# Where TensorE's idle transposes begin in a planned attention and MoE kernel, and separate order weights for its first and last units

## The chip, the cores and the metric

The kernel runs on one core of one Trainium2 chip. The core has a matrix engine (TensorE, PE), a vector engine (VectorE, DVE), an activation engine (ScalarE, ACT), a general engine (GpSimd, POOL) and an engine that here only issues transfers (SyncE, SP). The metric is the device time of one execution in microseconds. Three runs of the kernel before gave 693.09, 693.29 and 693.81 us, a median of 693.29.

## The reference

The computation is an attention whose queries are averaged in twos, followed by two MLPs without residuals. Everything is float32. The weights of the exponent are sharp, since q and k are scaled up by about 6 each.

```python
# q, k, v: (2, 8, 1152, 64)
q_pool = q.reshape(B, H, S // 2, 2, D).mean(axis=3)
scores = np.matmul(q_pool, k.transpose(0, 1, 3, 2)) / np.sqrt(D)
attn = np.exp(scores - scores.max(-1, keepdims=True))
attn = attn / (attn.sum(-1, keepdims=True) + 1e-09)
x = merge_heads(np.matmul(attn, v))                        # (1152, 512)
g = x @ w_gate                                             # d_ff 1536
x = (g * sigmoid(g) * (x @ w_val)) @ w_out
h = x @ w_in                                               # d_ff 2048
out = (np.maximum(h, 0) + alpha * np.minimum(h, 0)) @ w_out2
```

## The kernel before

**Numbers in two parts.** To keep float32's accuracy, every operand of a matmul is split into a high part (rounded to the type that PE multiplies at speed) and a low part (the rest). A product is then two or three matmuls. For the attention the splits are made on ACT, DVE and POOL; for the weights of the MLPs, `weights` (line 363) loads 1024 columns and runs seven steps on them: two on ACT (lines 376 and 381) and five on DVE (lines 377 to 380 and 382).

**Attention.** The 16 heads are handled as 8 pairs. A pair has 1152 pooled query rows, in 9 units of 128 (unit 4 holds the last rows of one head and the first of the other). For a unit, `unit` (line 513) computes scores against all 1152 keys, in three pieces of 448, 448 and 256 columns (line 542, PE), takes the row maximum on DVE (lines 551 and 552) and the exponents on ACT (lines 554 and 556). `transposed` (line 565) turns the exponents in three blocks of 384 with PE transposes (line 583). Each block is then split: either by ACT (line 605, high part) and DVE (line 606, low part), or, for every third block, by an ACT copy (line 591) and POOL (lines 601 and 602). `values` (line 611) multiplies with v (line 623), and `finish` (line 643) scales by the inverse sums and writes the attention's output in two parts, `xh` and `xl`. `prep` (line 402) loads and splits q, k and v for a pair. For the first pair it loads q in two pieces and k in three; q's second piece is needed from unit 2 on.

**MLPs.** `contract` (line 702) multiplies a block of weights with 384 tokens (line 710); then follow gating or the leaky step, and the output products (lines 770 and 798). Work of the first MLP on the first tokens needs only pairs 0 to 3, so it can run while the last pair of the attention is still under way.

**The order of the work.** Nothing of this order stands in the loops. Every piece of work is a task with an engine, an assumed duration and a priority, and `Plan.run` (line 122) plays the program through once while it is being built: each engine takes the ready task with the lowest priority number whose buffers have a place, and the instructions are emitted in that order. At run time each engine keeps that order and waits by semaphores. Priorities count four per pair: unit `n` of pair `p` has position `4p + 4(n + 0.5)/9`, and to it an offset from the dictionary `KNOB` (line 24) is added: `qk` for scores, `max` for the maxima, `exp` for the exponents, `t` for the transposes, `hi` and `lo` for the parts, `v` for the products, `prep` and `fin` for a pair's begin and end. Tasks of a weight block have the priority `max(clock - lead, floor)`, where the clock starts at 33 behind the last pair. `begin` names the unit of the last pair before whose transposes no weight of the MLPs is loaded. The `hold` numbers say how long an engine may stay idle for a more urgent task that is nearly ready.

**Idle transposes.** Ahead of the plan, PE does 21 transposes of the identity matrix (line 286). In the plan, as long as the planned time is under 40 us and no product has begun, a PE that has nothing ready does one more such transpose (line 289), for which the plan counts 0.109 us:

```python
free = {PE: 0.0, ACT: 0.0, DVE: 0.0, POOL: 1.7, SP: 0.6}
...
if e == PE and free[e] <= now + 1e-9 and now < 40.0 and not self.classes["acc"]["next"]:
    self.idle()
    free[e] = now + tp(P)
```

PE's planned time begins at 0. The 21 transposes ahead of the plan are not counted in it.

## Time and profile before

| | us |
|---|---|
| median of three runs | 693.29 |
| the profiled execution | 692.54 |
| its span (first to last instruction) | 690.7 |
| PE busy | 680.7 (99%) |
| DVE busy | 524.4 (76%) |
| ACT busy | 391.1 (57%) |
| POOL busy | 216.1 (31%) |

The profile is that of one execution. Its times start at the span's start. "Busy" on PE includes transposes that compute nothing, and matmuls are pipelined, so that PE's busy time covers small gaps. PEld is the loading of weights into PE, which overlaps the matmuls. A row of a timeline names a start, a duration, an engine, a line, an operation and, in brackets, how long the engine was idle before and for whom.

### The profile page before, as it was taken

The page shows a single profiled execution, that of the slowest core. Times are in us where ns is not written, and L with a number is a line of the kernel's source. Part 1 is how long each engine was busy: PE and PEld are TensorE (multiplying, and loading weights), DVE is VectorE, ACT ScalarE, POOL GpSimd, SP SyncE. Part 2 cuts the span into 40 slices and gives each one's busy share as a digit, 9 for nine tenths or more (in the row PEclk, how much of TensorE's full clock was granted, in tenths as well). Part 3 has the DMA queues.
Part 4 walks back from the last instruction along what each step waited for, and adds up shares of the span by engine and source line. Part 5 has one row for each costly group of instructions (what it writes and reads, how often), then busy time and mean ns, then how long its engine had stood idle before and what let it go on. Part 6 is the DMA issues. An engine that isn't in the chain of part 4 may idle for free.

```text
span 690.7 us, 11125 instructions
## 1 busy us (share of the span) xinstructions
PE 680.7 (99%) x4108; PEld 640.7 (93%) x4108; DVE 524.4 (76%) x900; ACT 391.1 (57%) x833; POOL 216.1 (31%) x246
## 2 busy tenths in 40 slices
PE   9999999999999989999999999999999999999997
PEld 8899999999999979999999999998999998999886
DVE  3798988889889899999775696659699559663432
ACT  2888889998998985545433442231376464342210
POOL 2879698898987751000000000004200000000000
PEclk9999999999999999999999999999999999999999
DMA  6665566664664233434331132013113303000012
GB/s 184 173 135 145 135 163 167 156 156 118 158 154 112 89 124 140 164 139 156 139 134 62 61 122 86 38 61 122 62 62 122 122 1 121 1 1 1 1 47 91
DMA packets 21655, 72.99 MB, mean 106 GB/s; under 512 B 3096, under 2 KB 4064, under 8 KB 21600
## 3 DMA queue, kind: packets, MB, share of 16 engines
q1 hardware_dynamic: 21312, 71.92, 34.3%
q8 instruction: 32, 0.52, 0.3%
q10 hardware_dynamic: 288, 0.36, 0.1%
q14 instruction: 23, 0.19, 0.1%
HBM read 52.17 MB, written 2.40 MB: 79 GB/s over the span
## 4 chain that ended last, share of the span: by engine, by line
PE 89%; DVE 8%; POOL 1%; issue 1%; ACT 0%; DVEq 0%; POOLq 0%
PE bank L710 35%; PE bank L798 14%; PE bank L542 12%; PE bank L583 10%; PE bank L623 10%; PE bank L770 7%; PE bank L289 1%; DVE fed L606 1%; POOL xh L779 1%; DVE plain L777 1%; DVE magnitudes L379 1%; DVE stats L551 1%; DVE weights L382 1%; DVE magnitudes L377 1%; DVE xl L780 1%
## 5 line engine op out<-in xcount | busy, mean ns | idle before, releaser
L710 PE MATMUL bank<-xh,weights 128*128 128x384 f32 x960 | 253.5, 337 | 0.5 <-DVE plain L777 0.3
L710 PEld LDWEIGHTS bank<-xh,weights 128*128 128x128 f32 x960 | 174.4, 188 | 2.4 <-issue 0.6
L710 PE MATMUL bank<-xl,weights 128*128 128x384 f32 x480 | 161.4, 336 | 0.0
L623 PE MATMUL bank<-fed 128*128 128x256 f32 (+1 forms) x576 | 109.5, 310 | 1.0 <-POOL fed L602 0.6
L583 PE MATMUL bank<-ident,plain 128*128 128x128 f32 x648 | 102.3, 275 | 2.1 <-DVE fed L606 1.4
L798 PE MATMUL bank<-fed 128*128 128x512 f32 x432 | 102.6, 389 | 0.0
L542 PE MATMUL bank<-fed 128*128 128x448 f32 (+3 forms) x396 | 100.9, 360 | 0.4 <-ACT plain L556 0.4
L606 DVE TENSOR_TENSOR fed<-bank,fed 128x384 fp32r<-128x384 f32 (+1 forms) x176 | 82.1, 496 | 16.2 <-ACT fed L605 14.7
L798 PEld LDWEIGHTS bank<-fed 128*128 128x128 f32 x432 | 80.6, 188 | 14.9
L710 PEld LDWEIGHTS bank<-xl,weights 128*128 128x128 f32 x480 | 90.2, 188 | 1.0
L583 PEld LDWEIGHTS bank<-ident,plain 128*128 128x128 f32 x648 | 76.4, 140 | 12.7 <-DVE fed L606 5.8
L623 PEld LDWEIGHTS bank<-fed 128*128 128x128 f32 x576 | 84.2, 189 | 3.2 <-POOL fed L602 1.0
L551 DVE TENSOR_REDUCE stats<-bank 128x1 f32<-128x896 f32 x72 | 78.1, 1085 | 10.2 <-PE bank L542 9.1
L605 ACT ACTIVATE fed<-bank 128x384 fp32r<-128x384 f32 (+1 forms) x176 | 72.2, 453 | 16.2 <-PE bank L583 15.7
L770 PE MATMUL bank<-fed 128*128 128x384 f32 x432 | 80.3, 337 | 0.9 <-DVE plain L777 0.8
L770 PEld LDWEIGHTS bank<-fed 128*128 128x128 f32 x432 | 75.6, 188 | 2.4 <-DVE plain L777 2.4
L779 POOL TENSOR_SCALAR xh<-plain 128x384 fp32r<-128x384 f32 x12 | 12.3, 1027 | 207.8 <-DVE plain L777 207.8
L556 ACT ACTIVATE plain<-bank,stats 128x896 f32<-128x896 f32 x72 | 73.1, 1015 | 0.3
L602 POOL TENSOR_TENSOR fed<-plain,fed 128x384 fp32r<-128x384 f32 x64 | 71.5, 1118 | 5.3
L542 PEld LDWEIGHTS bank<-fed 128*128 128x128 f32 (+1 forms) x396 | 63.2, 189 | 5.9 <-ACT plain L556 2.1
L750 ACT ACTIVATE plain<-bank,signs 128x384 f32<-128x384 f32 x48 | 28.0, 582 | 68.3 <-PE bank L710 68.3
L751 DVE SCALAR_TENSOR_TENSOR plain<-bank,signs,plain 128x384 f32<-128x384 f32 x48 | 29.4, 615 | 36.3 <-ACT plain L750 36.3
(73 smaller groups left out, 838.4 us busy)
## 6 DMA issues: line engine op xcount, KB each, us to landing
fed<-fed SPq DMA_DIRECT2D x60, 288.0 KB, 3.4
plain<-in_w_out SPq DMA_DIRECT2D x28, 512.0 KB, 4.1
plain<-in_w_in SPq DMA_DIRECT2D x16, 512.0 KB, 4.3
plain<-in_w_gate SPq DMA_DIRECT2D x12, 512.0 KB, 3.4
plain<-in_w_val SPq DMA_DIRECT2D x12, 512.0 KB, 4.6
plain<-in_vt SPq DMA_DIRECT2D x8, 576.0 KB, 5.8
plain<-in_qt SPq DMA_DIRECT2D x7, 576.0 KB, 7.2
plain<-in_kt SPq DMA_DIRECT2D x7, 576.0 KB, 7.6
```

The lines of the kernel that those rows point to most:

```text
L542: nc.tensor.matmul(bank[:, banks[i], :js.stop - js.start], l(), r(js), start=a == 0, stop=a == len(terms) - 1)
L551: add(DVE, dve(2 * WIDE), lambda: nc.vector.tensor_reduce(m(1), two(), AX.XY, ALU.min), pos + K["max"], [(sa, 0), (sa, 1)], [(st, 1)], [sa ...
L556: add(ACT, act(2 * WIDE, acc=True), lambda: nc.scalar.activation(e.ap[:, :2 * WIDE].rearrange("p (a b) -> p a b", a=2), two(), AF.Exp, bia ...
L583: nc.tensor.transpose(t.ap[:, c * P:c * P + P], e.ap[:, ks:ks + P], ident)
L602: add(POOL, gp2(BLK * w), lambda cp=cp, to=to, cols=cols: nc.gpsimd.tensor_tensor(to(1), src3(cp.ap)[:, :, cols], to(0).bitcast(F32), ALU. ...
L605: add(ACT, act(BLK * w), lambda t=t, to=to, cols=cols: nc.scalar.activation(to(0), src3(t.ap)[:, :, cols], AF.Copy), at + K["hi"], [t], [( ...
L606: add(DVE, dve(BLK * w), lambda t=t, to=to, cols=cols: nc.vector.tensor_tensor(to(1), src3(t.ap)[:, :, cols], to(0).bitcast(F32), ALU.subt ...
L623: nc.tensor.matmul(acc.ap[:, :n], v, b.ap[:, at:at + n], start=kc == 0 and part == 0, stop=kc == NK - 1 and part == 1)
L710: nc.tensor.matmul(acc.ap[:, :TB], l[:, cs], r[:, c, ts], start=c == 0 and a == 0, stop=c == KC - 1 and a == 2)
L751: add(DVE, dve(TB) + 0.056, lambda: nc.vector.scalar_tensor_tensor(u.ap, a.ap[:, :TB], sign(), u.ap, ALU.mult, ALU.max), prio, [a], [u], [ ...
L770: nc.tensor.matmul(acc.ap[:, :TB], l[:, os_], r, start=n == 0 and m == 0, stop=n == len(g) - 1 and m == 2)
L798: nc.tensor.matmul(acc.ap, l, r, start=n == 0 and m == 0, stop=n == len(g) - 1 and m == 2)
```

## The change

- PE's planned time begins at 5.0 (`first`) instead of 0.0.
- A function `turn` gives the tasks of unit 0 of pair 0 (`ramp=1`), and of unit 8 of the last pair (`last=1`), an extra offset in the order (`qk0` and so on, `qk9` and so on). The products have an extra offset for the first two groups of pair 0 (`v0`) and for the last two groups of the last pair (`v9`).
- In the last pair, POOL takes every second block instead of every third (`pool9=2`, `pooln=9`).
- The low part of the first `wlo` weight blocks can be made on POOL; `wlo` is 0.
- The base offsets and holds of `KNOB` have new values, among them `exp` (1.119 to 1.755), `lo` (-4 to -1.847), `begin` (1 to 0), `lead` (2.5 to 5.556) and `floor` (32.203 to 32.61).

```diff
--- before.py
+++ after.py
@@ -21,7 +21,7 @@
-KNOB = dict(qk=-1.541, max=-1.328, exp=1.119, t=-0.493, hi=-1.499, lo=-4, v=1.588, prep=-0.504, fin=0.163, hold_pe=0.2, hold_act=0.017, hold_dve=0, hold_pool=0.228, pvn=1, begin=1, lead=2.5, floor=32.203, warm=21, wide=448, tb=(5, 6, 2), ab=(7,), pool=3, e=3, et=6, wc=3, wr=4, h=17)
+KNOB = dict(ramp=1, qk0=-0.057, max0=1.439, exp0=1.712, t0=-0.168, hi0=-0.613, lo0=1.449, v0=-0.09, last=1, qk9=-0.348, exp9=2.109, t9=-0.81, hi9=-0.422, lo9=-1.681, v9=-2.742, pool9=2, pooln=9, wlo=0, qk=-1.546, max=-1.339, exp=1.755, t=-0.488, hi=-1.801, lo=-1.847, v=1.584, prep=-0.593, fin=0.029, hold_pe=0.192, hold_act=0, hold_dve=0.009, hold_pool=0.13, pvn=1, begin=0, lead=5.556, floor=32.61, warm=21, wide=448, tb=(5, 6, 2), ab=(7,), pool=3, e=3, et=6, wc=3, wr=4, h=17)
 class Task:
@@ -51,6 +51,7 @@
     def __init__(self):
         self.tasks = []
         self.classes = {}
+        self.first = 5.0
         self.idle = None
         self.wr = {}
         self.rd = {}
@@ -122,7 +123,7 @@
     def run(self, hold):
         self.held = set()
-        free = {PE: 0.0, ACT: 0.0, DVE: 0.0, POOL: 1.7, SP: 0.6}
+        free = {PE: self.first, ACT: 0.0, DVE: 0.0, POOL: 1.7, SP: 0.6}
         wait = {e: [] for e in free}
         moved = 2.6
         events, seq = [], 0
@@ -360,6 +361,8 @@
     LEAST = 3.4332275390625e-05
+    made = [0]
+
     def weights(kind, srcs, prio):
         raw, mag, w = buf("raw"), buf("mag"), buf(kind)
         for i, src in enumerate(srcs):
@@ -379,7 +382,9 @@
         add(DVE, dve(2 * DM), lambda: nc.vector.scalar_tensor_tensor(bits(), word(0, I32), 29, bits(), ALU.logical_shift_right, ALU.bitwise_or), prio, reads=got, writes=[mag], bufs=[raw, mag])
         add(DVE, dve(2 * DM), lambda: nc.vector.scalar_tensor_tensor(bits(), word(1, I32), -0x40000000, bits(), ALU.bitwise_and, ALU.bitwise_or), prio, reads=got, writes=[mag], bufs=[raw, mag])
         add(ACT, act(2 * DM, True), lambda: nc.scalar.activation(hi(), mag.ap, AF.Copy), prio, reads=[mag], writes=[w], bufs=[mag, w])
-        add(DVE, dve(2 * DM), lambda: nc.vector.tensor_tensor(w.ap[:, 2 * DM:], mag.ap, hi().bitcast(F32), ALU.subtract), prio, reads=[mag], writes=[w], bufs=[mag, w])
+        made[0] += 1
+        lo, dur, eng = (POOL, gp2(2 * DM), nc.gpsimd) if made[0] <= K["wlo"] else (DVE, dve(2 * DM), nc.vector)
+        add(lo, dur, lambda: eng.tensor_tensor(w.ap[:, 2 * DM:], mag.ap, hi().bitcast(F32), ALU.subtract), prio, reads=[mag], writes=[w], bufs=[mag, w])
         return [(w, i) for i in range(len(srcs))]
     def whi(u):
@@ -401,6 +406,7 @@
     def prep(p):
         x = Pair()
+        x.p = p
         s0 = 4.0 * (p - 1) + K["prep"]
         first = p == 0
         x.qq, x.kk = [None, None], [None, None]
@@ -509,6 +515,15 @@
         return x
     count = [0]
+
+    def turn(kind, p, n):
+
+
+        if p == 0 and n < K["ramp"]:
+            return K[kind] + K.get(kind + "0", 0.0)
+        if p == NP - 1 and n >= 9 - K["last"]:
+            return K[kind] + K.get(kind + "9", 0.0)
+        return K[kind]
     def unit(x, p, n, pos):
@@ -543,18 +558,18 @@
         for i in range(3):
             s = sb if i == 2 else sa
-            add(PE, len(terms) * mm(CUTS[i][1] - CUTS[i][0]), lambda i=i: scores(i), pos + K["qk"], rd(CUTS[i]), [(s, i)], [s] + held)
+            add(PE, len(terms) * mm(CUTS[i][1] - CUTS[i][0]), lambda i=i: scores(i), pos + turn("qk", p, n), rd(CUTS[i]), [(s, i)], [s] + held)
         m = lambda i: st.ap[:, i:i + 1]
         sum_ = lambda i: x.sums.ap[:, i, n:n + 1]
         two = lambda: bank[:, first:first + 2, :WIDE]
         one = lambda: bank[:, 2, :S - 2 * WIDE]
-        add(DVE, dve(2 * WIDE), lambda: nc.vector.tensor_reduce(m(1), two(), AX.XY, ALU.min), pos + K["max"], [(sa, 0), (sa, 1)], [(st, 1)], [sa, st])
+        add(DVE, dve(2 * WIDE), lambda: nc.vector.tensor_reduce(m(1), two(), AX.XY, ALU.min), pos + turn("max", p, n), [(sa, 0), (sa, 1)], [(st, 1)], [sa, st])
         add(DVE, dve(S - 2 * WIDE) + 0.056, lambda: nc.vector.tensor_scalar(junk[:, :S - 2 * WIDE], one(), m(1), None, ALU.min, ALU.min, accum_out=m(0)),
-            pos + K["max"], [(st, 1), (sb, 2)], [(st, 0)], [sb, st])
+            pos + turn("max", p, n), [(st, 1), (sb, 2)], [(st, 0)], [sb, st])
         add(ACT, act(S - 2 * WIDE, acc=True), lambda: nc.scalar.activation(e.ap[:, 2 * WIDE:], one(), AF.Exp, bias=m(0), scale=-1.0, accum_out=sum_(0)),
-            pos + K["exp"], [(st, 0), (sb, 2)], [(e, 1), (x.sums, n, 0)], [sb, e, st, x.sums])
+            pos + turn("exp", p, n), [(st, 0), (sb, 2)], [(e, 1), (x.sums, n, 0)], [sb, e, st, x.sums])
         add(ACT, act(2 * WIDE, acc=True), lambda: nc.scalar.activation(e.ap[:, :2 * WIDE].rearrange("p (a b) -> p a b", a=2), two(), AF.Exp, bias=m(0), scale=-1.0, accum_out=sum_(1)),
-            pos + K["exp"], [(st, 0), (sa, 0), (sa, 1)], [(e, 0), (x.sums, n, 1)], [sa, e, st, x.sums])
+            pos + turn("exp", p, n), [(st, 0), (sa, 0), (sa, 1)], [(e, 0), (x.sums, n, 1)], [sa, e, st, x.sums])
         return e, [[(e, h) for h in range(2) if (i * TB < 2 * WIDE if h == 0 else (i + 1) * TB > 2 * WIDE)] for i in range(NBLK)]
@@ -582,13 +597,13 @@
                     ks = (i * BLK + c) * P
                     nc.tensor.transpose(t.ap[:, c * P:c * P + P], e.ap[:, ks:ks + P], ident)
-            add(PE, tp(BLK * P), tr, at + K["t"], etok[i], [t] + mark, [t, e])
+            add(PE, tp(BLK * P), tr, at + turn("t", p, n), etok[i], [t] + mark, [t, e])
             src3 = lambda ap: ap[:, :BLK * P].rearrange("p (c q) -> p c q", q=P)
             c0 = 0
-            by_pool = K["pool"] and blocks[0] % K["pool"] == 0 and n != 4
+            by_pool = n != 4 and (blocks[0] % K["pool"] == 0 if p < NP - 1 else n < K["pooln"] and blocks[0] % K["pool9"] == 0)
             if by_pool:
                 cp = buf("cp")
-                add(ACT, act(BLK * P), lambda t=t, cp=cp: nc.scalar.activation(cp.ap, t.ap[:, :BLK * P], AF.Copy), at + K["hi"], [t], [cp], [t, cp])
+                add(ACT, act(BLK * P), lambda t=t, cp=cp: nc.scalar.activation(cp.ap, t.ap[:, :BLK * P], AF.Copy), at + turn("hi", p, n), [t], [cp], [t, cp])
             for et, off, w, width in dst:
                 b = et[i]
@@ -598,19 +613,20 @@
                 cols = slice(c0, c0 + w)
                 if by_pool:
-                    add(POOL, gp(BLK * w), lambda cp=cp, to=to, cols=cols: nc.gpsimd.tensor_scalar(to(0), src3(cp.ap)[:, :, cols], 1.0, 1.0, ALU.mult, ALU.mult), at + K["hi"], [cp], [(b, off, 0)], [cp, b])
+                    add(POOL, gp(BLK * w), lambda cp=cp, to=to, cols=cols: nc.gpsimd.tensor_scalar(to(0), src3(cp.ap)[:, :, cols], 1.0, 1.0, ALU.mult, ALU.mult), at + turn("hi", p, n), [cp], [(b, off, 0)], [cp, b])
                     add(POOL, gp2(BLK * w), lambda cp=cp, to=to, cols=cols: nc.gpsimd.tensor_tensor(to(1), src3(cp.ap)[:, :, cols], to(0).bitcast(F32), ALU.subtract),
-                        at + K["lo"], [cp, (b, off, 0)], [(b, off, 1)], [cp, b])
+                        at + turn("lo", p, n), [cp, (b, off, 0)], [(b, off, 1)], [cp, b])
                 else:
-                    add(ACT, act(BLK * w), lambda t=t, to=to, cols=cols: nc.scalar.activation(to(0), src3(t.ap)[:, :, cols], AF.Copy), at + K["hi"], [t], [(b, off, 0)], [t, b])
+                    add(ACT, act(BLK * w), lambda t=t, to=to, cols=cols: nc.scalar.activation(to(0), src3(t.ap)[:, :, cols], AF.Copy), at + turn("hi", p, n), [t], [(b, off, 0)], [t, b])
                     add(DVE, dve(BLK * w), lambda t=t, to=to, cols=cols: nc.vector.tensor_tensor(to(1), src3(t.ap)[:, :, cols], to(0).bitcast(F32), ALU.subtract),
-                        at + K["lo"], [t, (b, off, 0)], [(b, off, 1)], [t, b])
+                        at + turn("lo", p, n), [t, (b, off, 0)], [(b, off, 1)], [t, b])
                 b.parts += [(b, off, 0), (b, off, 1)]
                 c0 += w
     def values(x, g, et, eo, xs, pos):
         j, q0, q1 = GROUPS[g]
         n = q1 - q0
+        later = K["v"] + (K["v0"] if x.p == 0 and g < 2 else K["v9"] if x.p == NP - 1 and g > 1 else 0.0)
         acc = buf("acc")
         for kc in range(0, NK, K["pvn"]):
             b = et[kc // BLK]
@@ -622,10 +638,10 @@
                         at = (part * BLK + kc % BLK) * n
                         nc.tensor.matmul(acc.ap[:, :n], v, b.ap[:, at:at + n], start=kc == 0 and part == 0, stop=kc == NK - 1 and part == 1)
-            add(PE, 2 * K["pvn"] * mm(n), pv, pos + kc * 0.007 + K["v"], b.parts + [(x.vs[j], 0), (x.vs[j], 1)], [acc], [acc, b, x.vs[j]])
+            add(PE, 2 * K["pvn"] * mm(n), pv, pos + kc * 0.007 + later, b.parts + [(x.vs[j], 0), (x.vs[j], 1)], [acc], [acc, b, x.vs[j]])
         mine, rest = (slice(0, D), slice(D, P)) if j == 0 else (slice(D, P), slice(0, D))
-        add(ACT, act(n) + 0.136, lambda: nc.scalar.activation(eo.ap[mine, q0:q1], acc.ap[rest, :n], AF.Copy), pos + K["v"], [acc], [(eo, g)], [acc, eo])
-        add(DVE, dve(n), lambda: nc.vector.tensor_tensor(xs.ap[mine, q0:q1], acc.ap[mine, :n], eo.ap[mine, q0:q1], ALU.add), pos + K["v"], [acc, (eo, g)], [(xs, g)], [acc, eo, xs])
+        add(ACT, act(n) + 0.136, lambda: nc.scalar.activation(eo.ap[mine, q0:q1], acc.ap[rest, :n], AF.Copy), pos + later, [acc], [(eo, g)], [acc, eo])
+        add(DVE, dve(n), lambda: nc.vector.tensor_tensor(xs.ap[mine, q0:q1], acc.ap[mine, :n], eo.ap[mine, q0:q1], ALU.add), pos + later, [acc, (eo, g)], [(xs, g)], [acc, eo, xs])
     def inverses(x, pos, rd):
```

## Rows read from the trace of the kernel before

**Rows 1.** The page: busy time, and the chain that ended last by engine.

```profile
PE 680.7 (99%) x4108; PEld 640.7 (93%) x4108; DVE 524.4 (76%) x900; ACT 391.1 (57%) x833; POOL 216.1 (31%) x246
...
PE 89%; DVE 8%; POOL 1%; issue 1%; ACT 0%; DVEq 0%; POOLq 0%
```

**Rows 2.** Busy us by stage: length, PE, PEld, DVE, ACT, POOL, clock, DMA, GB/s.

```profile
5.00:11.86 6.86, 6.86 (x64) 6.70 (x62) 2.48 (x6) 2.13 (x5) 1.49 (x4) 1.00 0.96 285
44.00:226.00 182.00, 181.74 (x1297) 169.15 (x1296) 162.34 (x353) 163.94 (x438) 151.94 (x169) 1.00 0.58 144
226.00:235.00 9.00, 9.00 (x70) 8.55 (x70) 7.43 (x16) 7.98 (x23) 6.08 (x8) 1.00 0.37 129
235.00:269.00 34.00, 30.91 (x203) 27.63 (x201) 33.28 (x55) 27.10 (x58) 18.48 (x17) 1.00 0.34 123
269.00:455.00 186.00, 186.00 (x1069) 185.96 (x1070) 145.25 (x209) 76.14 (x115) 0.92 (x1) 1.00 0.30 111
455.00:489.00 34.00, 32.83 (x182) 31.04 (x181) 27.86 (x41) 7.40 (x8) 11.81 (x11) 1.00 0.20 71
```

**Rows 3.** The chain of waits from 0 to 30 us (start, us, what).

```profile
5.17 6.77 PE bank L289 x62
11.93 0.79 PE bank L542 x3
...
15.36 1.35 PE bank L289 x11
```

**Rows 4.** The timeline of 0 to 14 us (start, us, engine, operation).

```profile
5.55 0.42 DVE L450 SCALAR_TENSOR_TENSOR fed<-plain,fed 128x256 fp32r<-128x256 f32 x1 [0.48 <-ACT fed L446]
6.02 1.59 DVE L458 TENSOR_TENSOR fed<-plain,fed 128x448 fp32r<-128x448 f32 x3
...
8.05 0.47 ACT L446 ACTIVATE fed<-plain 128x320 fp32r<-128x320 f32 x1 [1.29 <-DVE plain L445]
...
13.82 1.09 DVE L551 TENSOR_REDUCE stats<-bank 128x1 f32<-128x896 f32 x1 [5.81 <-PE bank L542]
```

**Rows 5.** The timeline, 12 to 20 us: q's second piece, its copy.

```profile
14.83 0.48 DVE L450 SCALAR_TENSOR_TENSOR fed<-plain,fed 128x320 fp32r<-128x320 f32 x1
...
15.34 1.10 SPq L491 DMA_DIRECT2D fed<-fed  x2
```

**Rows 6.** Groups by shape over the whole run (busy us, mean ns).

```profile
L606 DVE TENSOR_TENSOR fed<-bank,fed 128x384 fp32r<-128x384 f32 x128 | 67.8, 550 | 12.0 <-ACT fed L605 10.8 <-PE bank L583 0.6
...
L289 PE MATMUL bank<-ident 128*128 128x128 f32 x83 | 10.3, 275 | 0.0
```

**Rows 7.** Waits, 40 to 226 us (total us, times, longest).

```profile
PEld bank L583 <- DVE fed L606: 2.8, 13, 0.3
```

**Rows 8.** Groups from 226 to 262 us, then two over the whole run.

```profile
L602 POOL TENSOR_TENSOR fed<-plain,fed 128x384 fp32r<-128x384 f32 x9 | 12.0, 1330 | 0.8
...
L601 POOL TENSOR_SCALAR fed<-plain 128x384 fp32r<-128x384 f32 x9 | 6.9, 762 | 9.7 <-ACT plain L591 9.7
...
L379 DVE SCALAR_TENSOR_TENSOR magnitudes<-plain,magnitudes 128x1024 int32<-128x1024 int32 x2 | 3.0, 1490 | 0.0
L377 DVE TENSOR_SCALAR magnitudes<-magnitudes 128x1024 f32<-128x1024 f32 x3 | 2.9, 952 | 0.0
...
L379 DVE SCALAR_TENSOR_TENSOR magnitudes<-plain,magnitudes 128x1024 int32<-128x1024 int32 x34 | 42.2, 1242 | 0.2
...
L377 DVE TENSOR_SCALAR magnitudes<-magnitudes 128x1024 f32<-128x1024 f32 x34 | 24.2, 712 | 6.7 <-ACT magnitudes L376 6.3
```

**Rows 9.** The timeline of POOL from 226 to 262 us.

```profile
228.36 1.01 POOL L602 TENSOR_TENSOR fed<-plain,fed 128x384 fp32r<-128x384 f32 x1
...
256.19 1.94 POOL L602 TENSOR_TENSOR fed<-plain,fed 128x384 fp32r<-128x384 f32 x1
```

**Rows 10.** Busy time, first and last of three stretches, 13 to 16 us.

```profile
13.00:14.00 1.00, 1.00 (x7) 0.95 (x8) 0.18 (x1) 0.00 (x0) 0.00 (x0) 1.00 0.00 0
...
15.00:16.00 1.00, 1.00 (x8) 0.71 (x7) 1.00 (x4) 0.25 (x1) 0.60 (x2) 1.00 0.00 0
```

## The prediction

> **What bounds the kernel now.** The page comes first: TensorE (PE) is busy for 680.7 us of a span of 690.7 and carries 89% of the chain that ended last, VectorE (DVE) 8% [rows 1]. A PE that is "99% busy" still says nothing about how much of that work is needed, so the next view is the busy time by stage [rows 2]. The reader is to see five stages. From 269 to 455 us PE has no idle time at all, and from 44 to 226 us (pairs 1 to 6 of the attention) it has 0.26 us: there only less PE work would help. Between 235 and 269 us PE has 3.09 us idle while DVE works 33.28 of 34 us: the passage into the first MLP is bound by DVE. Between 455 and 489 PE is idle for 1.17 us. And the stretch from 5 to 11.86 us is full of PE work in which nothing is computed: the chain of waits has 62 idle transposes in a row, 6.77 us from 5.17 on, and the first scores only behind them at 11.93 [rows 3].
>
> Are the scores late because their operands are? The timeline of the start says no [rows 4]. The low part of the first piece of q is done at 5.55 + 0.42 = 5.97 us; the three low parts of k take 1.59 us from 6.02, so the first is there at about 6.02 + 0.53 = 6.55 and the last at 7.61. The first scores could start near 6.6 us and start 5.3 us later. The plan's PE begins at time 0 and sends a transpose every 0.109 us until the planned operands are ready; the real PE first does 21 transposes of the preamble, so all 62 come late. DVE's first maximum (13.82 us) and all that follows hang on these scores.
>
> **The change, part by part.**
>
> *PE of the plan starts at 5.0.* In the plan 62 steps of 0.109 us reach from 0 to 6.76, so the operands are ready there between 6.65 and 6.76. From 5.0 that takes 16 or 17 steps: 45 or 46 transposes go, at 6.77 / 62 = 0.1092 us each [rows 3] 4.91 to 5.02 us; I take 4.95. The last of the 16 ends at 5.17 + 16 x 0.1092 = 6.92 us, 0.35 us behind the first operands, so nothing waits there. Next in line are the second and third pieces: three score matmuls take 0.79 us [rows 3], so the second piece is wanted at about 7.7 us and all three low parts are done by 7.61. Then comes the second piece of q: its ACT half ends at 8.05 + 0.47 = 8.52 [rows 4], its DVE half (0.48 us) ran at 14.83 only because it stood behind the first maximum [rows 5]; the queue copy that reads it left at 15.34. Both can move by the whole 4.95. If DVE does this piece ahead of the maximum, the maximum is late by some 0.2 us once. Bounds: 5.3 us at best (all that the operands allow), and 2.9 at worst (the transfer rival below).
>
> *Weights of unit 0 of pair 0 (`qk0` to `lo0`).* They reorder one unit of 72, inside a ramp that has 21 more idle transposes (83 in all [rows 6] less the 62), 11 of them in one run at 15.36 [rows 3]: 21 x 0.1092 = 2.3 us is all they could give. The most that they could cost is one maximum put behind another, 1.0 us (14.83 - 13.82 between two DVE starts). I take 0.
>
> *Base weights and holds.* In the steady pairs the order on DVE and ACT is set by distances of several units; a unit is 0.444 in the order, and `qk`, `max`, `t`, `v` move by under 0.02. `lo` moves from -4 to -1.85, still ahead of `max` (-1.34) for a unit up to one behind; `exp` was last on ACT and still is. Their price is bounded by the waits that reordering can remove or double: PE's weight loads wait 2.8 us for DVE's low parts over 40 to 226 us [rows 7]. I take 0, with 2 us either way.
>
> *The last pair: every second block by POOL.* Blocks 1, 3, 5, ... 27 without those of unit 4 make 12, against 8 now. Four subtractions at 0.55 us leave DVE [rows 6], 2.2 us; ACT's copy replaces ACT's rounding. They come back as four POOL blocks: a rounding and a subtraction, 0.762 + 1.330 = 2.09 us in this stretch [rows 8]. POOL has room: 6.08 + 18.48 = 24.56 us busy [rows 2], against the 36 us from 226 to about 262 in which the attention ends; with 4 x 2.09 it is 32.9. But the two engines slow each other: the 1024-element DVE steps of the weights take 0.952 and 1.490 us there against 0.712 and 1.242 over the whole run [rows 8], 3 x 0.24 + 2 x 0.25 = 1.2 us lost beside 9 blocks, 0.14 a block, so 0.5 us for four. Net 2.2 - 0.5 = 1.7 us of DVE time. Half of the four blocks fall before 235 us, where DVE is not full (7.43 of 9 us [rows 2]), so I count 1.1 us. Bounds: a gain of 3.09 us, all of PE's idle time in the stage, and a loss of 4.2 (the port rival).
>
> Two rows bear on a rule here. A POOL subtraction took 1.01 us at 228.36, before any weight was converted, and 1.94 us at 256.19, beside DVE's steps on the weights [rows 9]. The Trainium skill (SBUF — State Buffer, section "Who interferes with whom") says that VectorE and GpSimd share one port pair, held for a whole instruction, and that the loser blocks fully. These rows agree in direction; the mean loss of DVE, 0.14 us a block, is far below full blocking. By the rule the four blocks would stop DVE for all of their time, which is the port rival.
>
> *Loads begun at unit 0, `lead`, `floor`, last-pair weights.* The loads of the MLP's weights may start one unit earlier, and their conversion stands a little later in the order. DVE is full from 235 us on, so the order inside that stretch moves work but does not remove it; an earlier start can use the 1.57 us that DVE has free from 226 to 235. I count nothing beyond the 1.1. SP issues the same transfers. `wlo` is 0: that branch changes nothing. In the second passage `lead` can win or lose PE's idle 1.17 us [rows 2]; I take 0.
>
> **Sum.** The profiled execution took 692.54 us, 1.84 beside its span of 690.7. 692.54 - 4.95 - 1.1 = 686.5. It lies 0.75 us below the median of the runs, 693.29; on that scale the forecast is 693.29 - 6.05 = **687.2 us**.
>
> **The rivals.**
>
> *All of it works.* The start gives 5.0, the passage into the MLP its 3.09 and the ramp 1.2: 693.29 - 9.3 = 684.0. For it: DVE alone is full in that passage. Against it: less than 2.2 us are taken from DVE.
>
> *Transfers eat part of the start.* From 5 to 11.86 us the DMA engines are 0.96 busy [rows 2]; what follows is pulled onto them 4.95 us earlier. Against it: they rest in the three stretches of 1 us from 13 to 16 us [rows 10], a pause that takes 3 us of the pull. What is left costs 4.95 - 3 = 2 us: with 1.1 from the passage, 689.2.
>
> *The port.* The four added blocks hold DVE for their undisturbed time, 1.01 us for the subtraction and, in the same proportion, 0.762 x 1.01 / 1.33 = 0.58 for the rounding: 4 x 1.59 = 6.4 us. Less the 2.2 taken off, DVE is 4.2 us later in the passage that it bounds: 693.29 - 4.95 + 4.2 = 692.5, no change. For it: the stretched rows. Against it: the nine blocks of now cost DVE 1.2 us and not 9 x 1.59 = 14.3.
>
> *POOL becomes the bound, and the kernel slower.* Its place is the last pair: 13 blocks instead of 9 in 226 to 262 us and 24.56 - 9 x 2.09 = 5.7 us of other work. If every subtraction takes the 1.94 us and the rounding stretches alike, a block is 2.09 x 1.94 / 1.33 = 3.05 us: POOL needs 13 x 3.05 + 5.7 = 45.4 us in a stretch of 36, and PE's products wait 9.4 us: 693.29 - 4.95 + 9.4 = 697.7. It makes the kernel slower by over 1.4 us from (36 + 4.95 + 1.4 - 5.7) / 13 = 2.8 us a block on; the mean is 2.09 now.
>
> **How the numbers follow.** Forecast 0.61 (its own range 685.4 to 688.8), all of it works 0.14, transfers 0.10, port 0.10, POOL 0.05. Differences of under 0.2%, 1.4 us, cannot be told from none, so "faster" is below 691.9. The first three cases are faster (0.85), and of the port's 0.10 some 0.02 lie below 691.9: 0.87, 0.08, 0.05. The range runs from 684.4 to 690.2: it leaves out the port, POOL, and a third of the best case.
>
> **What would show it.** Right: a run of 16 or 17 idle transposes instead of 62, first scores at 6.9 us, the first maximum near 8.9, and each pair's end 5 us earlier; 12 POOL blocks in the last pair, under 2.4 us each; PE's idle time in the passage at about 2 us instead of 3.09. Wrong: scores that wait for k or q behind the transposes, a gain of 5 us at 12 us that has shrunk by 45 us, steady pairs longer by a few tenths each, or products that wait for POOL at the end of the last pair.

## Result, and the profile after

The changed kernel takes 697.83 us (median of 4, 697.20 to 699.15) beside 693.33 us for the kernel before: a ratio of 1.0069 [1.0057, 1.0081], 4.5 us slower. The forecast was 687.2. The profiled execution took 698.2 us with a span of 696.4.

The page after (engine busy time; then the chain that ended last, by engine):

```profile
PE 680.1 (98%) x4062; PEld 636.3 (91%) x4062; DVE 533.0 (77%) x896; ACT 391.4 (56%) x833; POOL 222.6 (32%) x254
...
PE 77%; DVE 12%; POOL 4%; issue 3%; ACT 2%; DMA 1%; SPq 0%; DVEq 0%; POOLq 0%; ACTq 0%
```

PE has 46 instructions fewer than in [rows 1], as the change says, and its share of the chain fell from 89 to 77%. DVE (12% for 8) and POOL (4% for 1) took over half of what PE lost. The chain at the start (start, us, what):

```profile
1.35 4.74 PE bank L287 x21
6.09 2.31 PE bank L290 x16
8.40 0.80 PE bank L557 x3
```

There are 16 idle transposes instead of 62, and the first scores come at 8.40 us instead of 11.93 [rows 3]: 4.46 us less of idle transposes, and 0.93 us given back ahead of them, where the preamble's 21 transposes took 4.74 us. In the profile before they ended at 5.17, where [rows 3] begins. In both traces the first transposes begin 0.21 us apart and later ones 0.109 us apart. This step comes at about 4.1 us before and at about 7.1 us after, behind five of the idle ones, which is why the 16 took 2.31 us and not 1.75. One microsecond shows it, before and then after (columns as in [rows 2]; the granted clock is 1.00 in both, so it does not say why):

```profile
4.50:5.50 1.00, 1.00 (x12) 1.00 (x10) 0.42 (x1) 0.40 (x2) 0.00 (x0) 1.00 1.07 387
```

```profile
4.50:5.50 1.00, 1.00 (x7) 1.00 (x6) 0.52 (x2) 0.69 (x2) 0.00 (x0) 1.00 1.06 350
```

Then the steady pairs. First the kernel after, then the kernel before; columns as in [rows 2]:

```profile
40.00:226.00 186.00, 181.49 (x1278) 165.84 (x1277) 167.13 (x347) 162.30 (x433) 150.75 (x167) 1.00 0.56 140
...
226.00:241.00 15.00, 14.38 (x107) 13.56 (x107) 12.05 (x24) 14.06 (x36) 12.37 (x16) 1.00 0.43 114
241.00:275.00 34.00, 29.44 (x192) 26.35 (x191) 32.65 (x51) 24.28 (x53) 21.05 (x20) 1.00 0.36 124
461.00:495.00 34.00, 32.79 (x182) 31.00 (x182) 27.86 (x42) 7.39 (x8) 11.79 (x11) 1.00 0.21 71
```

```profile
40.00:226.00 186.00, 185.74 (x1325) 172.83 (x1324) 165.93 (x360) 167.89 (x447) 155.49 (x173) 1.00 0.58 144
```

PE's idle time rises from 0.26 to 4.51 us, but the count says more: 1278 PE instructions in 186 us where there were 1325. At 186 / 1325 = 0.140 us each, 47 instructions are an estimated 6.6 us of work, and PEld's busy time fell by 7.0 us. In the passage into the MLP PE is idle for 0.62 + 4.56 = 5.18 us from 226 to 275, against 3.09 [rows 2]. The last passage is unchanged (1.21 against 1.17). So −4.46 + 0.93 + 6.6 + 2.1 = +5.2 us, and the spans differ by 5.7.

What is most visibly longer in a pair is one operation of DVE: `xl`, the low part of a finished pair's output, a subtraction with two operands in SBUF. Its rows in the timeline after, pairs 0 to 7, and then before, pairs 1 to 7 (start, us):

```profile
65.12 1.59 DVE L670 TENSOR_TENSOR xl<-plain,xh 128x576 fp32r<-128x576 f32 x1
94.92 1.93 DVE L670 TENSOR_TENSOR xl<-plain,xh 128x576 fp32r<-128x576 f32 x1
125.54 1.91 DVE L670 TENSOR_TENSOR xl<-plain,xh 128x576 fp32r<-128x576 f32 x1
...
217.54 1.92 DVE L670 TENSOR_TENSOR xl<-plain,xh 128x576 fp32r<-128x576 f32 x1
247.42 1.96 DVE L670 TENSOR_TENSOR xl<-plain,xh 128x576 fp32r<-128x576 f32 x1 [0.90 <-POOL xh L669]
276.33 0.75 DVE L670 TENSOR_TENSOR xl<-plain,xh 128x576 fp32r<-128x576 f32 x1
```

```profile
99.17 0.98 DVE L654 TENSOR_TENSOR xl<-plain,xh 128x576 fp32r<-128x576 f32 x1
128.63 0.99 DVE L654 TENSOR_TENSOR xl<-plain,xh 128x576 fp32r<-128x576 f32 x1
...
216.98 0.97 DVE L654 TENSOR_TENSOR xl<-plain,xh 128x576 fp32r<-128x576 f32 x1
241.00 0.75 DVE L654 TENSOR_TENSOR xl<-plain,xh 128x576 fp32r<-128x576 f32 x1
270.99 0.74 DVE L654 TENSOR_TENSOR xl<-plain,xh 128x576 fp32r<-128x576 f32 x1
```

The starts also give the length of a pair: (217.54 − 94.92) / 4 = 30.66 us after, (216.98 − 99.17) / 4 = 29.45 before. Why the same subtraction takes twice as long is seen when DVE and POOL stand side by side. After, around pair 2's end, DVE, then POOL, then PE:

```profile
127.38 0.55 DVE L621 TENSOR_TENSOR fed<-bank,fed 128x384 fp32r<-128x384 f32 x1
...
125.41 1.43 POOL L514 TENSOR_TENSOR fed<-plain,fed 128x576 fp32r<-128x576 f32 x1
...
127.98 0.87 PE L598 MATMUL bank<-ident,plain 128*128 128x128 f32 x6 [0.72 <-DVE fed L621]
```

`xl` starts at 125.54, 0.13 us behind POOL's subtraction of v (L514, 125.41 to 126.84), and ends at 127.45, 0.61 us behind that subtraction's end. Nothing is left of the overlap: the 1.91 us are POOL's remaining 1.30 and most of the 0.75 that `xl` takes alone. The low part of a block of exponents (L621) stands behind it, and PE waits 0.72 us for that. Before, the order on DVE was another: `xl` came behind one more maximum and one more low part, when POOL's subtraction had ended, and met only POOL's short rounding of a block (L601):

```profile
127.16 1.09 DVE L551 TENSOR_REDUCE stats<-bank 128x1 f32<-128x896 f32 x1
128.17 0.55 DVE L606 TENSOR_TENSOR fed<-bank,fed 128x384 fp32r<-128x384 f32 x1
...
126.71 1.42 POOL L508 TENSOR_TENSOR fed<-plain,fed 128x576 fp32r<-128x576 f32 x1
128.50 0.52 POOL L601 TENSOR_SCALAR fed<-plain 128x384 fp32r<-128x384 f32 x1 [0.37 <-ACT plain L591]
129.10 1.40 POOL L602 TENSOR_TENSOR fed<-plain,fed 128x384 fp32r<-128x384 f32 x1
```

Here too `xl` (128.63 to 129.62) ends 0.60 us behind the POOL instruction that it began behind, and POOL's next subtraction, which began under `xl`, takes 1.40 us instead of 1.01. In every trace where the subtraction `xl` began behind an instruction of POOL, it ended 0.60 to 0.64 us behind that one's end, however much of it was left.

From 40 to 226 us after, PE's weight loads wait 10.7 us for DVE's low parts, where [rows 7] has 2.8, and its transposes themselves another 4.1 (the two can overlap):

```profile
PEld bank L598 <- DVE fed L621: 10.7, 25, 1.0
...
PE bank L598 <- DVE fed L621: 4.1, 6, 0.8
```

The Trainium skill (SBUF — State Buffer, section "Who interferes with whom") states the rule that fits: VectorE reaches its second SBUF operand by a port pair shared with GpSimd, locked by one of them for a whole instruction. The trace agrees for this operation: 1.91 us, ending 0.61 us behind POOL.

### The profile page after: what moved, and what is told of

The parts are those of the page before. It is cut to its first block, busy times and chain, and to the rows that moved or that the text cites. A ratio compares the mean times of both kernels' runs of the same rounds, so it can differ in the third digit from the quotient of the medians.

```text
span 696.4 us, 11025 instructions
## 1 busy us (share of the span) xinstructions
PE 680.1 (98%) x4062; PEld 636.3 (91%) x4062; DVE 533.0 (77%) x896; ACT 391.4 (56%) x833; POOL 222.6 (32%) x254
## 4 chain that ended last, share of the span: by engine, by line
PE 77%; DVE 12%; POOL 4%; issue 3%; ACT 2%; DMA 1%; SPq 0%; DVEq 0%; POOLq 0%; ACTq 0%
PE bank L726 35%; PE bank L814 14%; PE bank L557 7%; PE bank L786 7%; PE bank L598 6%; PE bank L639 6%; DVE fed L621 3%; DVE stats L566 2%; POOL fed L617 1%; DVE junk L567 1%; DMA plain<-in_vt 1%; DVE xl L670 1%; POOL xh L795 1%; POOL fed L616 1%; DVE plain L793 1%
## 5 line engine op out<-in xcount | busy, mean ns | idle before, releaser
L639 PE MATMUL bank<-fed 128*128 128x256 f32 (+1 forms) x576 | 107.4, 308 | 2.7 <-DVE fed L621 1.6
L621 DVE TENSOR_TENSOR fed<-bank,fed 128x384 fp32r<-128x384 f32 (+1 forms) x172 | 80.2, 495 | 15.4 <-ACT fed L620 14.3
L620 ACT ACTIVATE fed<-bank 128x384 fp32r<-128x384 f32 (+1 forms) x172 | 70.4, 450 | 22.4 <-PE bank L598 21.9
L617 POOL TENSOR_TENSOR fed<-plain,fed 128x384 fp32r<-128x384 f32 x68 | 73.0, 1074 | 5.7
```

Source lines behind the costliest of these rows:

```text
L617: add(POOL, gp2(BLK * w), lambda cp=cp, to=to, cols=cols: nc.gpsimd.tensor_tensor(to(1), src3(cp.ap)[:, :, cols], to(0).bitcast(F32), ALU. ...
L620: add(ACT, act(BLK * w), lambda t=t, to=to, cols=cols: nc.scalar.activation(to(0), src3(t.ap)[:, :, cols], AF.Copy), at + turn("hi", p, n) ...
L621: add(DVE, dve(BLK * w), lambda t=t, to=to, cols=cols: nc.vector.tensor_tensor(to(1), src3(t.ap)[:, :, cols], to(0).bitcast(F32), ALU.subt ...
L639: nc.tensor.matmul(acc.ap[:, :n], v, b.ap[:, at:at + n], start=kc == 0 and part == 0, stop=kc == NK - 1 and part == 1)
```

## The experiments

The theory: the start gives its 5 us, the base weights lose them again by putting `xl` under POOL's subtraction of v, and the last pair's settings cost a little. The rivals: the new order itself is slower, or the early start exhausts a transfer and cannot be kept.

**The start alone.** The kernel before with one number changed.

```
- free = {PE: 0.0, ACT: 0.0, DVE: 0.0, POOL: 1.7, SP: 0.6}
+ free = {PE: 5.0, ACT: 0.0, DVE: 0.0, POOL: 1.7, SP: 0.6}
```

> The kernel before with PE's planned time begun at 5.0 and nothing else changed: the same order on every engine, 16 idle transposes ahead of the first scores instead of 62. Theory (the start pays what was forecast, and the loss of the changed kernel comes from the new order weights in the steady pairs): 46 x 0.109 = 5.0 us less, 688.3; 689.3 if the 21 transposes of the preamble take 4.74 us, as in the changed kernel, and not 3.81. The gain of 4 to 5 us at the first scores stays unchanged to the end, and every pair keeps its 29.5 us. Rival (an engine order that is run 5 us earlier meets transfers and buffers that are late, and loses about 1.1 us a pair): no gain, 693 to 698, with pairs of 30.6 us.

Measured: 687.84 us, 0.9928 [0.9916, 0.9939], some 5.2 us gained. The steady pairs are as before (its busy time from 40 to 226 us):

```profile
40.00:226.00 186.00, 185.75 (x1329) 173.15 (x1327) 166.02 (x360) 167.08 (x448) 155.65 (x173) 1.00 0.56 141
```

So the start term stood, and it is kept to the end. The loss is in the rest of the change.

**`xl` with one operand in SBUF** (changed kernel; the low part's value is left out, in this and the other kernel with one operand):

```
- nc.vector.tensor_tensor(xl[:, pp, ts], xs.ap, xh[:, pp, ts].bitcast(F32), ALU.subtract)
+ nc.vector.tensor_scalar(xl[:, pp, ts], xs.ap, tiny, None, ALU.min, ALU.min, accum_out=dummy)
```

> The changed kernel with the same order on every engine; the low part of a pair's output (VectorE, one task a pair) is made from one SBUF operand, a minimum with a column of a constant with an accumulated result, instead of a subtraction of two SBUF operands. This leaves the low part's value out. Theory (the subtraction starts 0.12 us after POOL's subtraction of v and is blocked by it, 1.92 us instead of 0.75, and the low parts of the next block behind it on VectorE hold PE up): the task takes about 0.75 to 0.85 us, each of the 7 pairs gets back about 1.1 us: 690 to 691. Rival (it is the place of the task ahead of the next block's low part that costs, whatever its length; the blocking is incidental): at most a third of it, 695.5 or more.

Measured: 692.50, 1.0001 [0.9987, 1.0015]. At the same place under POOL's subtraction it takes 0.81 us (DVE, then POOL):

```profile
122.15 0.81 DVE L671 TENSOR_SCALAR_CACHE_REDUCE xl<-plain,tiny 128x576 fp32r<-128x576 f32 x1
...
122.88 0.55 DVE L622 TENSOR_TENSOR fed<-bank,fed 128x384 fp32r<-128x384 f32 x1
...
122.03 1.44 POOL L515 TENSOR_TENSOR fed<-plain,fed 128x576 fp32r<-128x576 f32 x1
```

The place and the partner are the same and the order of every engine is that of the changed kernel; 5.3 us come back over all pairs. Up to 0.75 us of it is another gain: in pair 6 this form does not read `xh` and waits 0.15 us instead of 0.90. The form differs from the subtraction in its operation as well as in the second operand. The next row of DVE tells these apart: the low part of a block (L622) is a subtraction too, but one operand lies in PSUM (`bank`), and under the same subtraction of POOL it takes 0.55 us, its mean in [rows 6]. So for a subtraction it is the second operand in SBUF that is blocked.

**`xl` moved out from under POOL.** In the changed kernel `xl` is made to read a low part of the next pair (in all pairs but the last; the rest of the edit is left out here):

```
+ if p and n == 5:
+     low([(ets[2][1], HALF, 1)])
```

> The changed kernel with the low part of a pair's output put three places later on VectorE, behind the maximum and the low part of the next pair's unit 5, block 1; nothing is left out. Theory: POOL's subtraction of v is over by then, the low parts come in time, the pairs are 29.5 us again: 690 to 691.5. Rival (the loss of 1.1 us a pair comes from other order weights, such as the rounding on ACT or the holds): 696 to 698.

Measured: 698.47, 1.0075 [1.0061, 1.0089]: a miss. `xl` took 0.75 us in most pairs and PE did 1313 instructions from 40 to 226 us, but the added condition also re-ordered the last two pairs, and the passage lost what the pairs had gained. So it was repeated without pair 6 (`if 0 < p <= 6`, counted by the next pair; pair 0's `xl` did not change its place by it):

> The changed kernel; on VectorE the low part of a pair's output stands three places later for pairs 1 to 5, and nothing else differs in the order of any engine (in the run before it, the last two pairs had been reordered as well). Theory (POOL's subtraction of v blocks it at its old place): the five subtractions take 0.75 us instead of 1.92, five pairs get back 1.1 us each: 691.5 to 693. Rival (the pairs lose by the other order weights, and the run before was no faster for that reason): 697 to 698.5.

Measured: 693.37, 1.0000 [0.9991, 1.0009]; `xl` stands three DVE steps later and takes 0.76 us:

```profile
125.64 0.76 DVE L671 TENSOR_TENSOR xl<-plain,xh 128x576 fp32r<-128x576 f32 x1
```

4.5 us come back, 0.9 us for each of five pairs. This was not the move alone that was expected: in the traces the low part and the maximum behind `xl` have changed places too in these five pairs; the orders of the other engines are the same. A pure move in the finished order, which leaves those two as they were, and for pair 6 as well:

```
...
+ dve_ = [j for j in range(i + 1, len(emits)) if emits[j][0] == DVE]
+ emits.insert(dve_[2], emits.pop(i))        # pairs 1 to 6
```

> The changed kernel; on VectorE alone the low part of a pair's output stands three places later for pairs 1 to 6 (xl_behind_5 left pair 6 at its place, where it took 1.96 us in the profile), and no other instruction moves. Theory (each blocked subtraction costs 0.9 to 1.1 us, in the last pair too): 1 us less than xl_behind_5, 692 to 693. Rival (in the last pair the weights' steps fill VectorE anyway and the block is free): 693 to 694.

Measured: 693.08, 0.9999 [0.9990, 1.0008]: 4.75 us come back, so the move does it without the exchange. `xl` takes 1.02 us in pairs 1 to 5 here. Pair 6's still took 1.74 us, since it began 0.31 us behind the start of POOL's subtraction of v again; what freeing it would give is not shown.

**The converse: `xl` earlier in a kernel that has not the other changes.** The start-alone kernel, `xl` of pairs 1 to 5 two DVE steps earlier, ahead of a maximum and a low part (in the changed kernel the low part comes first):

```
...
+ dve_ = [j for j in range(i) if emits[j][0] == DVE]
+ emits.insert(dve_[-2], emits.pop(i))
```

> The kernel before with PE's planned time begun at 5.0 (687.8 us), and on VectorE alone the low part of a pair's output two places earlier for pairs 1 to 5, ahead of a maximum and a low part, as the changed kernel has it; every other engine's order is untouched. Theory: it now starts while POOL's subtraction of v runs, takes 1.6 to 1.9 us instead of 0.98, and holds the maximum and the low part up: 5 x 1.0 us, 692 to 694. Rival (the place on VectorE is harmless, and the changed kernel loses by something else in its pairs): 687.5 to 688.5.

Measured: 697.49, 1.0053 [1.0041, 1.0066]. A loss as large as that of the whole change is made by moving five instructions: 9.65 us above the start alone, 1.9 a pair, twice what was expected. `xl` takes 1.57 us:

```profile
125.13 1.57 DVE L660 TENSOR_TENSOR xl<-plain,xh 128x576 fp32r<-128x576 f32 x1
...
124.67 1.42 POOL L514 TENSOR_TENSOR fed<-plain,fed 128x576 fp32r<-128x576 f32 x1
```

To divide these 9.65 us, the same order with the one-operand form:

> The run start_xl_early with the low part of a pair's output made from one SBUF operand (a minimum with a column of a constant, with an accumulated result), which leaves its value out; the order of all engines is that of start_xl_early. Theory: with one SBUF operand POOL does not block it, it takes 0.8 us: 687.5 to 689. Rival (the earlier place costs by its order alone): within 1 us of start_xl_early.

Measured: 693.65, 1.0001 [0.9993, 1.0010]; the operation took 0.81 us. Missed: of the loss, 3.8 us are the block, and 5.8 us are the place itself, an unblocked 0.8 us put ahead of a maximum and a low part. PE's weight loads wait 8.1 us for the low parts there, and 2.6 in the start-alone kernel. In this kernel the rival, order, holds for more than half.

Does it cost anything that `xl` takes 0.98 us in the start-alone kernel? One place later in pairs 1 to 5, behind the next short minimum:

> The kernel before with PE's planned time begun at 5.0, and on VectorE the low part of a pair's output one place later for pairs 1 to 5, behind the short minimum. Theory: there it starts with POOL's subtraction of a block or ahead of it and takes 0.75 us instead of 0.98: up to 5 x 0.24 = 1.2 us less, 686.6 to 687.8. Rival (VectorE is not what bounds those pairs by then, POOL's subtraction waits instead): 687.8.

Measured: 688.28, 0.9924 [0.9912, 0.9937], no gain over 687.84. `xl` now begins first, and POOL is the one that is held (DVE, then POOL):

```profile
124.79 0.76 DVE L655 TENSOR_TENSOR xl<-plain,xh 128x576 fp32r<-128x576 f32 x1
...
124.85 1.58 POOL L602 TENSOR_TENSOR fed<-plain,fed 128x384 fp32r<-128x384 f32 x1
```

**One base weight at a time.** First `lo` of the changed kernel in the start-alone kernel:

```
- lo=-4
+ lo=-1.847
```

> The kernel before with PE's planned time begun at 5.0 (687.8 us) and one base weight of the changed kernel, lo = -1.847 instead of -4; all others as before. Theory (lo lets the low part of a pair's output pass the low part of a block, and there it runs into POOL's subtraction of v): pairs of 30 us or more with that subtraction at 1.4 us or more, 691 to 695. Rival (lo alone moves it to a place where POOL is elsewhere; it takes the other weights as well): 687 to 689.

Measured: 701.59, 1.0115 [1.0101, 1.0129], slower than either whole set. The wait that grew most is that of ACT's exponentials for DVE's short minima (`ACT plain L554 <- DVE junk L552`, 12.0 us from 40 to 226 against 4.1 in the start-alone kernel). Then the opposite, `lo=-4` in the changed kernel:

> The changed kernel (697.8 us) with lo = -4 again, all else as changed. Theory (lo is what moved the task): 690 to 693, the subtraction of a pair's output at 1.0 us or less. Rival (another base weight, exp, hi, fin or a hold, moves it): 696 to 699, still 1.9 us.

Measured: 708.72, 1.0222 [1.0208, 1.0236]. Both times missed. The mechanism did come in the first: `xl` took 1.59 to 1.61 us under POOL's subtraction of v in pairs 2 to 5, so `lo` alone is enough to put it there, but 13.75 us above the start alone is more than this block explains. In the second `xl` still took 1.39 us in pairs 2 and 4 and 0.75 in 1, 3 and 5. The weights are a set, and the division of the loss cannot be read off single ones.

**The last pair.** Its settings as before, in the changed kernel:

```
- last=1, ... v9=-2.742, pool9=2, ... begin=0, lead=5.556, floor=32.61
+ last=0, ... v9=0, pool9=3, ... begin=1, lead=2.5, floor=32.203
```

> The changed kernel with all settings of its last pair and of the weight loads as before: POOL takes every third block, no offsets for the last unit and the last products, begin 1, lead 2.5, floor 32.203. The pairs 0 to 6 keep the changed order. Theory (six of the seven blocked subtractions lie ahead of the last pair; from there on the changed kernel loses 2.3 us more, of which one more blocked subtraction is 1.1): 696.0 to 697.0, a gain of about 1.2. Rival (POOL's four added blocks are the main loss, as the port rival of the prediction had it: 4 to 6 us): 692 to 694.

Measured: 695.81, 1.0036 [1.0024, 1.0048]: 2.0 us come back. The opposite, the changed kernel with the base weights, holds and first unit of before, so that only the start and the last pair are changed:

> The changed kernel with all base weights and holds and the first unit's offsets as before: what is left of the change is PE's planned time begun at 5.0 and the settings of the last pair and of the weight loads (POOL takes every second block, begin 0, lead, floor, the offsets of the last unit and products). Pairs 0 to 6 then run as in start_alone (687.8 us). Theory (in last_back the last pair's settings cost 2.0 us): 689 to 691, with POOL's subtractions of blocks in the last pair stretched as before. Rival (the prediction: they gain 1.1): 686 to 687.2.

Measured: 689.96, 0.9944 [0.9932, 0.9957]: 2.1 us above the start alone. Both give the same price from either side. Pair 6's `xl` is in it (DVE, then POOL):

```profile
240.22 1.98 DVE L670 TENSOR_TENSOR xl<-plain,xh 128x576 fp32r<-128x576 f32 x1 [0.31 <-POOL xh L669]
...
240.15 1.44 POOL L514 TENSOR_TENSOR fed<-plain,fed 128x576 fp32r<-128x576 f32 x1
```

With both put back (`xl` later in pairs 1 to 5 by the pure move, last pair as before):

> The changed kernel with two repairs together: the low part of a pair's output three places later on VectorE for pairs 1 to 5, and the settings of the last pair and of the weight loads as before. Theory (the two losses lie in different stretches and add, 4.5 and 2.0 us of 697.8): 691 to 692; what is then left above start_alone (687.8), 3 to 4 us, belongs to the other base weights. Rival (they overlap, the last pair merely takes up delays of the pairs ahead): 693 to 694.

Measured: 692.33, 0.9989 [0.9980, 0.9997]: 5.5 us come back, where the two single runs add up to 6.5. Whether the two losses overlap is not shown, because the move is not the same as in the run that gave 4.5 us: beside the kernel with only the last pair put back, it gives 3.5 us for five instructions. The time is still 4.5 us above the start alone. Its waits from 40 to 226 us:

```profile
POOL fed L519 <- DMA plain<-in_vt: 9.1, 4, 2.5
PEld bank L604 <- DVE fed L627: 8.1, 20, 0.8
...
PE bank L604 <- DVE fed L627: 2.5, 6, 0.4
```

In the start-alone kernel the second of these is 2.6 us and the third is not there, so some of the low parts remain late, although `xl` (1.02 us here) is nearly out of the way. The first is 0.6 us there: in the changed order POOL's first rounding of v stands one block earlier in each pair, and waits for v's load. Which of these costs the time, and which base weight or which task of the first unit does it, was not isolated.

**A better version.** PE's planned start at 6.6 in the kernel before, the time at which the first operands were read to be ready:

```
- free = {PE: 0.0, ACT: 0.0, DVE: 0.0, POOL: 1.7, SP: 0.6}
+ free = {PE: 6.6, ACT: 0.0, DVE: 0.0, POOL: 1.7, SP: 0.6}
```

> The kernel before with PE's planned time begun at 6.6 instead of 0, nothing else: 2 idle transposes are left ahead of the first scores, which then wait only for k's low part, at 6.6 us. Theory: with the preamble ending at 5.2 to 6.1 us PE starts its scores at 6.7 to 6.9 instead of 7.0 to 7.9 us: 0.3 to 1.2 us less than start_alone, 686.6 to 687.5. Rival (with less work ahead of the scores PE's granted clock falls to its lower level and the first scores take twice as long): 689 or more.

Measured: 687.04, 0.9904 [0.9889, 0.9919], the fastest of all. Two of the 62 idle transposes are left, one ahead of the first scores and one behind them; the first scores start at 6.30 us, and the chain at the start is now q's own load:

```profile
0.72 4.16 DMA plain<-in_qt
...
6.30 1.13 PE bank L542 x3
```

## Why the prediction was wrong

**The start: right.** 46 transposes were to give 4.95 us; the start alone gave 5.2, and nothing was given back later. The rival "transfers eat part of the start" did not happen. The first scores came at 8.40 instead of 6.9, because the preamble took 0.93 us longer in that execution and the 16 idle transposes 2.31 us instead of 1.75.

**"Base weights and holds ... I take 0, with 2 us either way": this step failed.** With the rest of the change held, these weights and the first unit's cost 697.83 − 689.96 = 7.9 us. The step compared DVE's tasks with their neighbours on DVE (`lo` with `max` and `exp`) and asked by how many places each would move. It did not ask beside which instruction of another engine a moved task would run. It does not name `xl` at all. In pairs 1 to 5 the order on ACT stayed as it was, as the step said, but on DVE `xl` and a low part moved ahead of a maximum, two places for `xl`. Two tasks of POOL, one of DVE and two matmuls moved elsewhere in the pair, but on POOL `xh` and the subtraction of v that follows it kept their order. That put `xl` 0.13 us behind the start of POOL's subtraction of v, in five pairs alike. Of the 7.9 us, 3.5 to 5.3 are shown to be this: 3.5 and 4.75 by pure moves, 4.5 by a move with the exchange, and 5.3 by the one-operand form, which with the low parts under POOL says that the second operand in SBUF is the cause. Of the rest the traces show the waits above, and the cause is open. The bound of 2 us was read from waits that existed before [rows 7]; a bound on what can be removed is no bound on what can be added.

**The last pair: wrong sign.** +1.1 us of gain was taken; it costs 2.0 and 2.1 us in the two experiments. POOL did not become the bound: 13 blocks of 0.758 + 1.216 = 1.97 us, under the 2.4 that were to show it (groups of POOL from 231 to 267 us):

```profile
L617 POOL TENSOR_TENSOR fed<-plain,fed 128x384 fp32r<-128x384 f32 x13 | 15.8, 1216 | 1.1
L616 POOL TENSOR_SCALAR fed<-plain 128x384 fp32r<-128x384 f32 x13 | 9.9, 758 | 5.3 <-ACT plain L606 4.2 <-PE bank L639 1.1
```

They are quicker than the 2.09 of [rows 8]. That this rival's sum, 697.7 us, is nearly the measured time is chance, for what it describes did not happen. What the chain shows instead stands behind the blocks in POOL's line: the blocks put off the end of pair 6 on POOL, so that DVE waits 0.90 us for `xh` and is then blocked. The chain of the passage after shows it, and shows how a block looks in this view (start, us, what):

```profile
242.67 1.50 POOL fed L616
...
244.25 1.01 POOL fed L617
245.26 1.37 POOL plain L666
...
246.71 0.68 POOL xh L669
...
247.42 0.04 DVE xl L670
...
247.59 1.71 issue
249.31 1.14 DVE fed L621 x4
```

The 1.71 us of "issue" are DVE standing still inside `xl`: it waits for no semaphore, so the profile names no releaser. The start-last kernel has the same block (1.98 us) without these base weights, so it belongs to the last pair's settings. No run freed pair 6's `xl` alone, so how much of the 2 us this is was not measured.

**The port rival** had the mechanism, in the wrong place and with a chance of 0.10. It was dismissed by a mean, 0.14 us a block in the last pair. The five weight steps in this mean all met POOL's blocks in the trace before, and the price was not spread: three began ahead of the block's instruction and took 0.68, 0.67 and 1.21 us, two began behind it and took 1.50 and 1.77. Two of them, first ahead and then behind:

```profile
252.50 0.67 DVE L377 TENSOR_SCALAR magnitudes<-magnitudes 128x1024 f32<-128x1024 f32 x1
...
260.25 1.50 DVE L377 TENSOR_SCALAR magnitudes<-magnitudes 128x1024 f32<-128x1024 f32 x1
```

The 1.94 us of POOL in [rows 9] is such a meeting too: a step of DVE (L379) had begun 0.14 us ahead of it, took its usual 1.21 us, and POOL's subtraction ended 0.87 us behind that step. So POOL's blocks do not stop DVE for all of their time, as this rival had it, but only what begins behind them. Whoever began second paid in full; the mean was "far below full blocking" only because three of the five steps of DVE began first.

**What would show it wrong** did name the sign: "a gain of 5 us at 12 us that has shrunk by 45 us, steady pairs longer by a few tenths each". The steady pairs were longer, by 1.2.

## What to carry to other kernels

When a scheduler's weights change, lay the new order of each engine beside the order of the others at the few operations that share something, here VectorE's subtractions with two SBUF operands beside GpSimd's: a move of two places cost nearly 2 us a pair with all work unchanged. Split a change into its independent parts before it is judged; one number of this one (PE's planned start) gave 5 to 6 us, and the rest lost 10. In a kernel whose TensorE is 98% busy, compare instructions done in equal time and not busy shares: here 47 instructions fewer, some 6.6 us of work, showed as only 4.25 us more of idle time.

## What the runs showed of the hardware

- A DVE subtraction of 128x576 with two SBUF operands took 0.74 to 0.75 us alone, 0.97 to 0.99 when it began 0.13 us behind POOL's rounding of 0.51 us, and 1.91 to 1.98 when it began 0.07 to 0.13 us behind POOL's subtraction of 1.43 us. Its end then lay 0.60 to 0.64 us behind POOL's. When it began 0.06 us ahead, it kept its 0.76 and POOL's subtraction of 128x384 took 1.58 us instead of the 1.01 of [rows 9]. In these meetings the one that started first kept its usual time.
- The form with one SBUF operand and an accumulated result took 0.81 us under the same POOL subtraction, which took its usual 1.44. The low parts with one operand in PSUM took 0.55 us under it. But one operand in SBUF is not always safe: a step on the weights with one (L377) took 1.50 us when it began behind POOL's subtraction, and 0.67 when it began ahead.
- The preamble's 21 transposes, the same in all kernels, took from 3.81 us (before) to 4.74 (after) between executions, at a granted clock of 1.00 in the rows of both. They began 0.21 us apart up to some moment, about 4.1 us before and 7.1 us after (4.1 to 7.4 us over the sixteen traces), and 0.109 us from there on. With the 16 transposes behind them, 1.5 us of a comparison of two single traces was this.
- With two of the 62 idle transposes left at the start, PE waited 0.60 us between 5 and 8 us, and the granted clock over the whole kernel was 0.999.
